# Loading wq before the keys, and summing P V's masked blocks on another engine

## The chip, the core and the metric

The kernel runs on one core of a Trainium2 chip. The core has a matrix engine (TensorE, PE in the profile, with its weight loads as PEld), a vector engine (VectorE, DVE), a scalar engine (ScalarE, ACT), a general engine (GpSimd, POOL) and a queue processor that here only issues transfers (SyncE, SP). Each engine runs its own list of instructions in order and waits on semaphores for the others. Sixteen DMA engines move data between the memory (HBM) and the on-chip memory. The metric is the device time of one execution in microseconds. A change of 0.2% is about 0.39 us.

## What is computed

One decode step of a transformer block for 8 sequences (B), one token each. x has 512 features. The layer norm of x is multiplied by wq into 32 query heads of 128 features. Each group of four query heads shares one of 8 key-value heads. Only the last 2048 of 8192 cached positions count:

```python
q = (layernorm(x) @ wq).reshape(8, 32, 128)
k = k_cache[:, :, -2048:, :]       # per sequence and kv head: 2048 x 128
v = v_cache[:, :, -2048:, :]
p = softmax(q . k * 128**-0.5)     # 4 query heads per kv head
h = x + (p . v).reshape(8, 4096) @ wo
# then a mixer/MLP block; for one token its token mixing adds zero:
y = layernorm(h); x1 = y
out = h + x1 + gelu(layernorm(x1) @ w3) @ w4
```

The keys and values that count are 2 x 64 x 2048 x 128 bf16 numbers, 67 MB; wq and wo are 4.2 MB each, w3 and w4 1.8 MB each. Each byte is used once.

## The kernel before

**Loads.** All loads but x go through SP's queue, in an order written out as a string in lines 776 to 785. A letter K loads one group of keys: four kv heads of one sequence, 2 MB, so that each sequence has two groups; V does the same for values. There are 16 groups of each, three buffers for keys (`knat`) and three for values (`vnat`). SP runs through the list in order; a load of K's group j first waits until group j - 3 has been turned (`e_Thi`), a load of V's group m until the products with group m - 3 are done (`e_PV`). A wait holds up everything behind it on SP. Q loads wq (`load_wq`, line 759): one transfer of nearly all of it into `wbig`, and six small ones (the last 1152 columns of every fourth row of wq, 18 to 72 KB each) into `wqF`. Four of the six wait for a memset of POOL (line 217). wo, w3 and w4 come at the end of the list; the last group of V goes into a buffer of K.

**Work per key group.** Keys must be turned so that features lie on partitions. `pe_T(i)` (line 381 on) does that for one item, a quarter of a group: eight PE transposes into PSUM. `evict(i)` copies the result to `kT_sb`, the lower half on ScalarE (line 393), the upper half on VectorE (line 395). `pe_QK(i)` multiplies it with the queries, two turns later. The main loop (line 613) goes over 64 items p: turn item p, score item p - 2, and at fixed distances behind the last item of a sequence the steps of its softmax, the products with V (`pe_PV`, two per sequence) and the output (`pe_O`). Before the loop stand the turns of the first four items (group 0) and then `q_rows` (x times wq) and `q_turn` (queries turned and copied to `qT`); `fill(0)` and `fill(1)` on POOL spread the queries of the first two sequences into `qblk`, which the scores need.

**Work per value group.** `pe_PV(m)` multiplies the weights of four kv heads with the values in sixteen matmuls. Each result row holds four blocks of 128 features of which only one belongs to it. For all but the last sequence VectorE multiplies the 128x512 bank with a 0/1 mask into `omask` (line 514), and two GpSimd adds fold the four blocks into one (`acc`, lines 516 and 517): first two pairs, then the rest. The last sequence has its own form on VectorE (lines 519 to 523). `pe_O` waits for both groups of a sequence and is issued four to five turns later. `omask` has one buffer, so the mask of the next group waits for the adds of the one before.

Of the kernel before, what the change touches and what calls it, by code (L numbers as in the profile page):

```python
# [8 lines left out]
ALU = mybir.AluOpType  # L9
AX = mybir.AxisListType  # L10
# [69 lines left out]
def bass_sequential_preLN__sliding_block_cached__mixer_s_mlp__decode_kernel(  # L80
# [23 lines left out]
    with es:  # L104
# [57 lines left out]
        omask = sb([128, NS, DH], dt.float32, "omask")  # L162
# [40 lines left out]
        PE, AC, DV, PO, SP = (Engine(S(n)) for n in ("s_pe", "s_act", "s_dve", "s_pool", "s_sp"))  # L203
# [25 lines left out]
        e = DV.op(lambda e: e.bn_stats(st6[:, :], x_sb[:, :]), X)  # L229
        e = DV.op(lambda e: e.bn_aggr(mv[:, :], st6[:, :]), e)  # L230
        e = PO.op(lambda e: e.tensor_scalar(rstd[:, :], mv[:, 1:2], EPS, None, ALU.add), e)
        e = PO.op(lambda e: e.tensor_tensor(rstd[:, :], rstd[:, :], half[0:B, 0:1], ALU.pow), e)
# [8 lines left out]
        e = DV.op(lambda e: e.tensor_reduce(hsq[:, :], ident_f[:, :].rearrange("p (u h) -> p h u", u=4), AX.X, ALU.add))  # L241
# [21 lines left out]
        e = PE.op(pe_xT, e_xln, e_idb)  # L263
# [14 lines left out]
        def q_rows():  # L278
            for k, rows, n, at, where in fills():
                a = xln_b[:, :]  # L280
                cols = bass.AP(tensor=a.tensor, offset=a.offset + KC * at + KC - 1, ap=[a.ap[0], [KC, k], [KC * k, 4]])
                e_xP = DV.op(lambda e, cols=cols, where=where: e.tensor_copy(
                    xlnP[:, where].rearrange("b (e a) -> b e a", a=4), cols))

            def pe_fT(e):
                for k, rows, n, at, where in fills():
                    ins = e.matmul(fT_ps[rows, n * B:(n + 1) * B], xlnP[:, where], ident_b[0:B, 0:B],
                                   is_transpose=True, tile_position=(0, rows.start))
                return ins
            e = PE.op(pe_fT, e_xP)  # L290
            for k, rows, n, at, where in fills():
                e_fT = DV.op(lambda e, rows=rows, n=n: e.tensor_copy(xlnF[rows, n, 0:B], fT_ps[rows, n * B:(n + 1) * B]),
                             e, e_fz)
            out = []
            for j in range(2):
                def pe_q(e, j=j):
                    for kc in range(KC):
                        for u in range(4):
                            n = (4 * j + u) * R * DH
                            size = R * DH if kc < KC - 1 else max(0, min(R * DH, H * DH - QF - n))  # L300
                            if size:
                                ins = e.matmul(S_ps[j][32 * u:32 * (u + 1), 0:size], xlnT[:, kc, :], wq_v[:, kc, n:n + size],  # L302
                                               start=(kc == 0), stop=(kc == KC - 1 and size == R * DH),
                                               tile_position=(0, 32 * u), skip_group_check=True)
                    return ins

                def pe_qF(e):
                    for n in range(NF):
                        for u in range(4):
                            w = (u - 4) * R * DH + QF  # L310
                            lo = max(0, -w)
                            if lo < R * DH:
                                ins = e.matmul(S_ps[1][32 * u:32 * (u + 1), lo:R * DH], xlnF[:, n, :],
                                               wqF[:, n, w + lo:w + R * DH], start=False, stop=(n == NF - 1),
                                               tile_position=(0, 32 * u), skip_group_check=True)
                    return ins
                e_q = PE.op(pe_q, e_xT, (sem_wq, 16))
                if j == 1:
                    e_q = PE.op(pe_qF, e_fT, (sem_wf, 16 * len(FILL)))
                got = S_ps[j][:, :].rearrange("p (r d) -> p r d", r=R)  # L320
                for c in range(2):
                    if j == 0:
                        e = AC.op(lambda e, c=c, got=got: e.activation(qrow2[:, 0, :, c, :], got, ACT.Copy, scale=inv_sqrt_dh),
                                  e_q)
                    else:
                        e = DV.op(lambda e, c=c, got=got: e.tensor_scalar(qrow2[:, 1, :, c, :], got, inv_sqrt_dh, None,
                                                                          ALU.mult), e_q)
                out.append(e)
            return out, e_q

        def q_turn():
            e_qT = []
            for j in range(2):
                def f(e, j=j):
                    for r in range(R):
                        ins = e.matmul(qT_ps[j][:, r * 128:(r + 1) * 128],
                                       qrow2[:, j, r, :, :].rearrange("p c d -> p (c d)").bitcast(dt.float32), ident_f[:, :],
                                       start=True, stop=True, is_transpose=True)
                    return ins
                e = PE.op(f, e_qrow[j], e_idf)  # L340
                got = qT_ps[j][:, :].bitcast(dt.bfloat16).rearrange("p (r u x) -> p r u x", r=R, u=4)[:, :, :, 0:2 * B]
                e_qT.append(DV.op(lambda e, j=j, got=got: e.tensor_copy(  # L342
                    qT[:, 4 * j:4 * (j + 1), :, :, :].rearrange("p u r b e -> p r u (b e)"), got), e))
            return e_qT[-1], e
# [10 lines left out]
        pool = [e_oz]  # L355
# [3 lines left out]
        e_acc, e_O, e_oX, e_oW = ({} for _ in range(4))  # L359
# [95 lines left out]
        free = {2: None}  # L455
# [41 lines left out]
        def pe_PV(m):  # L497
            b, q = divmod(m, NQ)
            at, bank = bank_of(q)

            def f(e):
                for n in range(NN):
                    u = n % 2
                    ins = e.matmul(bank[64 * u:64 * (u + 1), :],  # L504
                                   pT_sb[:, b % 2, n, :].rearrange("p (x q) -> p q x", q=NQ)[:, q, :],
                                   v_tile(m)[:, n * 512:(n + 1) * 512], start=(n < 2), stop=(n >= NN - 2),
                                   tile_position=(0, 64 * u), skip_group_check=True)
                return ins
            e_PV[m] = PE.op(f, V(m), *(e_pT[b, x] for x in range(KQ)), free[at])
            acc = oacc[:, b % 2, q, :]  # L510
            if b < LAST:
                a = own_s[:, :]
                own = bass.AP(tensor=a.tensor, offset=a.offset, ap=[a.ap[0], [1, NS], [0, DH]])
                free[at] = DV.op(lambda e: e.tensor_tensor(omask[:, :, :], bank.rearrange("p (s d) -> p s d", s=NS), own,  # L514
                                                           ALU.mult), e_PV[m], e_acc.get(m - 1), e_own_s)
                e = PO.op(lambda e: e.tensor_tensor(omask[:, 0:2, :], omask[:, 0:2, :], omask[:, 2:4, :], ALU.add), free[at], pool[-1])  # L516
                pool[-1] = e_acc[m] = PO.op(lambda e: e.tensor_tensor(acc, omask[:, 0, :], omask[:, 1, :], ALU.add), e, e_O.get(b - 2))  # L517
                return
            e = DV.op(lambda e: e.tensor_scalar(acc, bank[:, 0:DH], own_s[:, 0:1], None, ALU.mult),
                      e_PV[m], e_O.get(b - 2), e_own_s)  # L520
            for s in range(1, NS):
                e = DV.op(lambda e, s=s: e.scalar_tensor_tensor(acc, bank[:, s * DH:(s + 1) * DH], own_s[:, s:s + 1], acc,
                                                                ALU.mult, ALU.add), e)
            e_acc[m] = free[at] = e
# [74 lines left out]
        def quad(f, q):  # L599
# [3 lines left out]
                   (5, each(widen, 2)), (5, each(warm, 1)), (5, each(widen, 3)), (6, each(warm, 2)), (6, each(warm, 1))),  # L603
                  ((6, quad(pe_PV, 0)), (7, quad(pe_PV, 1)), (11, late_O), (8, last_O)))
        LAG = (0, 0, 0, 0, 0, 0, KQ, -1)
        for p in range(AHEAD):
            pe_T(p)
            evict(p)
        e_qrow, e_q = q_rows()
        e_qT, e_qturn = q_turn()  # L610
        fill(0)
        fill(1)
        for p in range(NITEM + 24):
# [160 lines left out]
                B_w4[lo * 128:hi * 128, :].rearrange("(g p k) n -> p g (k n)", p=128, k=k), sem_w4[n])  # L774

        turn = {"K": 0, "V": 0, "O": 0}
        for kind in "KQKK" + 9 * "VK" + "VKKVKVKVVVOVOO":
            if kind == "Q":
                load_wq()
                continue  # L780
            {"K": load_k, "V": load_v, "O": load_wo}[kind](turn[kind])
            turn[kind] += 1
# [42 lines left out]
```

## Time and profile before

| | us |
|---|---|
| median of 3 runs | 193.28 (193.27 to 193.34) |
| the profiled execution, its own time | 193.18 |
| its span, first to last instruction | 191.9 |
| busy: PE, DVE, ACT, POOL | 151.5, 102.5, 95.7, 30.3 |
| share of the span in which 16 DMA engines moved queue 1's data | 97.2% |
| read from HBM | 79.18 MB |

In the profile a row of the timeline gives the start, the length, the engine, the line of the kernel, the operation, output<-input, the number of instructions merged into it, and in brackets how long the engine was idle before it and what ended that. A row of a group ends with total busy time, mean ns of one instruction, and the idle time before them. SPq rows are issues of transfers: they last as long as SP needs to issue, not as long as the data flow. A row "0.00:2.00 ..." of the table by stretches gives, for that stretch, the busy time of each engine, the clock that was granted to TensorE (1.00 is full), the mean share of the DMA engines and the rate.

### The profile page before, as it was taken

How to read it: one execution, taken by the hardware profiler on the slowest of the kernel's cores; microseconds unless marked ns; L12 is line 12 of the kernel's file. 1: busy time of each engine (PE TensorE's matmuls, PEld its weight loads, DVE VectorE, ACT ScalarE, POOL GpSimd, SP SyncE). 2: the span in 40 equal slices, each digit the busy share in tenths (PEclk: the TensorE clock that was granted, in tenths of full speed). 3: DMA queues.
4: the chain of work that ended last, by engine and by line, in shares of the span. 5: the costliest groups of instructions: out<-in, count | busy, mean ns of one | idle time of the engine just before them, and what ended most of it. 6: DMA issues, size and time to landing. Idle time of an engine off the chain costs nothing.

```text
span 191.9 us, 3209 instructions
## 1 busy us (share of the span) xinstructions
PE 151.5 (79%) x1325; PEld 94.9 (49%) x1325; DVE 102.5 (53%) x245; ACT 95.7 (50%) x124; POOL 30.3 (16%) x65
## 2 busy tenths in 40 slices
PE   0293879988878998699978896989898994777874
PEld 0281247664546555465655463746554661323453
DVE  2754314773386438543775275646853885535323
ACT  3081127776272927284559263754782767420331
POOL 8300020100230023002300230024002200140030
PEclk9999769999996999889999997999999999999985
DMA  6999999999999999999999999999999999999991
GB/s 220 422 406 432 437 420 427 434 437 424 434 429 427 430 430 427 429 430 430 437 430 420 437 430 429 420 437 424 437 434 425 434 434 432 408 430 428 411 409 75
DMA packets 6478, 79.38 MB, mean 414 GB/s; under 512 B 688, under 2 KB 704, under 8 KB 1856
## 3 DMA queue, kind: packets, MB, share of 16 engines
q1 hardware_dynamic: 6448, 79.18, 97.2%
q8 instruction: 10, 0.16, 0.3%
q14 instruction: 4, 0.03, 0.0%
q10 hardware_dynamic: 16, 0.01, 0.0%
HBM read 79.18 MB, written 0.01 MB: 413 GB/s over the span
## 4 chain that ended last, share of the span: by engine, by line
DMA 65%; PE 22%; DVE 6%; ACT 4%; SPq 1%; issue 1%; POOL 0%
DMA knat<-in_A_k_cache_dram 31%; DMA w_sb<-in_B_w_dram 16%; DMA vnat<-in_A_v_cache_dram 10%; PE kT_ps L383 9%; DMA wbig<-in_A_wq_dram 8%; PE S_ps L504 3%; ACT pT_sb L472 2%; PE S_ps L408 2%; PE o_rows L504 2%; DVE kT_sb L395 2%; ACT kT_sb L393 1%; PE S_ps L302 1%; PE sm L529 1%; PE kT_ps L678 1%; SPq L207 1%
## 5 line engine op out<-in xcount | busy, mean ns | idle before, releaser
L393 ACT ACTIVATE kT_sb<-kT_ps 128x1024 bf16<-128x1024 bf16 x64 | 65.6, 1025 | 65.3 <-PE kT_ps L383 65.2
L383 PE MATMUL kT_ps<-turn_f,knat 128*128 128x128 f32 x512 | 76.5, 293 | 12.2 <-DMA knat<-in_A_k_cache_dram 9.6
L383 PEld LDWEIGHTS kT_ps<-turn_f,knat 128*128 128x128 f32 x512 | 60.4, 149 | 31.9 <-issue 13.4
L395 DVE COPY kT_sb<-kT_ps 128x1024 bf16<-128x1024 bf16 x64 | 43.9, 686 | 34.7 <-PE kT_ps L383 34.6
L516 POOL TENSOR_TENSOR omask<-omask 128x256 f32<-128x256 f32 x14 | 10.2, 726 | 113.3 <-DVE omask L514 113.3
L408 PE MATMUL S_ps<-kT_sb,qblk 128*32 128x512 bf16 x256 | 26.5, 408 | 1.7 <-POOL qblk L350 1.1
L504 PE MATMUL o_rows<-vnat,pT_sb 128*64 128x512 bf16 x128 | 15.4, 381 | 5.4 <-ACT pT_sb L472 5.4
L472 ACT ACTIVATE pT_sb<-o_rows,own_f 128x512 bf16<-128x512 f32 x28 | 17.7, 694 | 1.8 <-PE o_rows L467 1.6
L504 PE MATMUL S_ps<-vnat,pT_sb 128*64 128x512 bf16 x112 | 13.4, 382 | 0.7 <-DMA vnat<-in_A_v_cache_dram 0.7
L504 PEld LDWEIGHTS o_rows<-vnat,pT_sb 128*64 128x64 bf16 x128 | 8.0, 109 | 11.5 <-issue 7.7
L408 PEld LDWEIGHTS S_ps<-kT_sb,qblk 128*32 128x32 bf16 x256 | 6.6, 93 | 13.4 <-issue 8.3
L514 DVE TENSOR_TENSOR omask<-o_rows,own_s 128x512 f32<-128x512 f32 x7 | 4.8, 686 | 12.5 <-PE o_rows L504 12.5
L514 DVE TENSOR_TENSOR omask<-S_ps,own_s 128x512 f32<-128x512 f32 x7 | 4.8, 692 | 11.7 <-PE S_ps L504 11.7
L350 POOL COPY qblk<-qT 64x64 bf16<-64x64 bf16 x16 | 5.0, 312 | 27.0 <-DVE qT L342 16.4
L504 PEld LDWEIGHTS S_ps<-vnat,pT_sb 128*64 128x64 bf16 x112 | 5.8, 110 | 6.8 <-issue 1.6
L529 PE MATMUL sm<-oacc,sel_o 128*128 128x256 f32 x16 | 7.2, 537 | 0.6 <-DVE oX L536 0.6
L440 ACT ACTIVATE E_sb<-S_ps,negM 128x512 f32<-128x512 f32 x8 | 5.5, 689 | 2.4 <-DVE negM L436 2.4
L259 PE MATMUL sm<-ident_b,xln_b 8*128 8x8 bf16 x4 | 0.3, 176 | 8.0 <-DVE xln_b L234 8.0
L517 POOL TENSOR_TENSOR oacc<-omask 128x128 f32<-128x128 f32 x14 | 6.4, 455 | 1.1
L559 ACT ACTIVATE orow<-kT_ps 128x512 bf16<-128x512 f32 x1 | 0.6, 597 | 11.2 <-PE kT_ps L553 11.2
L431 DVE TENSOR_REDUCE mblk<-S_ps 128x1 f32<-128x512 f32 x8 | 5.5, 682 | 0.8 <-PE S_ps L408 0.8
L453 DVE STREAM_TRANSPOSE PT_sb<-P_sb 128x512 bf16<-128x512 bf16 x8 | 5.6, 702 | 0.0
(120 smaller groups left out, 102.6 us busy)
## 6 DMA issues: line engine op xcount, KB each, us to landing
knat<-in_A_k_cache_dram SPq DMA_DIRECT2D x16, 2048.0 KB, 19.3
vnat<-in_A_v_cache_dram SPq DMA_DIRECT2D x15, 2048.0 KB, 20.3
wbig<-in_A_wq_dram SPq DMA_DIRECT2D x1, 3808.0 KB, 16.1
wbig<-in_A_wo_dram SPq DMA_DIRECT2D x2, 1024.0 KB, 22.9
knat<-in_A_v_cache_dram SPq DMA_DIRECT2D x1, 2048.0 KB, 20.4
wbig<-in_A_wo_dram SPq DMA_DIRECT2D x1, 2048.0 KB, 24.7
w_sb<-in_B_w_dram SPq DMA_DIRECT2D x1, 1792.0 KB, 30.7
w_sb<-in_B_w_dram SPq DMA_DIRECT2D x1, 1024.0 KB, 32.6
```

Of the source, the lines that this page charges most:

```text
L383: ins = e.matmul(kT_ps[i % 2][:, n * 256:(n + 1) * 256].bitcast(dt.float32), knat[:, j % NK, c * DH:(c + 2) * DH].bitcast(dt.float32), tur ...
L393: e_lo[i] = AC.op(lambda e: e.activation(kT_sb[:, i % NKT, 0:W // 2], kT_ps[i % 2][:, 0:W // 2], ACT.Copy), e_Tlo[i], e_QK.get(i - NKT))
L395: e_hi[i] = DV.op(lambda e: e.tensor_copy(kT_sb[:, i % NKT, W // 2:W], kT_ps[i % 2][:, W // 2:W]), e_Thi[i], e_QK.get(i - NKT))
L408: ins = e.matmul(S_ps[b % 2][32 * t:32 * (t + 1), :], qblk[:, b % 2, KQ * q + t, half, at:at + H], kT[:, :, t, :, half], start=(q == 0 and ...
L431: e = DV.op(lambda e: e.tensor_reduce(mblk[:, 0:1], S_ps[b % 2][:, :], AX.X, ALU.max), e_QK[G * b + G - 1], e_mz)
L453: e_PT[b] = DV.op(lambda e: e.transpose(PT_sb[:, :], P_sb[:, :]), e_P[b], e_wide.get(b - 1))
L472: e_pT[b, t] = AC.op(lambda e: e.activation(pT_sb[:, b % 2, :, H * t:H * (t + 1)], bank[:, :].rearrange("p (n y) -> p n y", n=NN), ACT.Cop ...
L504: ins = e.matmul(bank[64 * u:64 * (u + 1), :], pT_sb[:, b % 2, n, :].rearrange("p (x q) -> p q x", q=NQ)[:, q, :], v_tile(m)[:, n * 512:(n ...
L514: free[at] = DV.op(lambda e: e.tensor_tensor(omask[:, :, :], bank.rearrange("p (s d) -> p s d", s=NS), own, ALU.mult), e_PV[m], e_acc.get( ...
L516: e = PO.op(lambda e: e.tensor_tensor(omask[:, 0:2, :], omask[:, 0:2, :], omask[:, 2:4, :], ALU.add), free[at], pool[-1])
L517: pool[-1] = e_acc[m] = PO.op(lambda e: e.tensor_tensor(acc, omask[:, 0, :], omask[:, 1, :], ALU.add), e, e_O.get(b - 2))
L529: e_O[b] = PE.op(lambda e: e.matmul(O_ps, sel_o[:, :], oacc[:, b % 2, :, :].rearrange("p q d -> p (q d)"), start=True, stop=True), e_acc[N ...
```

## The change

Two edits. First, the list of loads starts with Q instead of K, so that wq and its six small transfers are issued ahead of K's group 0, and in the program `q_rows` and `q_turn` are emitted ahead of the turns and evictions of the first four items; on PE, ScalarE and VectorE the work on q therefore stands first. The loads behind the first eight stay in their order. Second, the four masked blocks are added by one VectorE reduce, which reads `omask` with the block index innermost (steps of 512 bytes) and writes `acc`, in place of the two GpSimd adds. GpSimd's later work (the fills, a memset near the end) no longer stands behind those adds.

```diff
@@ pe_PV
-                e = PO.op(lambda e: e.tensor_tensor(omask[:, 0:2, :], omask[:, 0:2, :], omask[:, 2:4, :], ALU.add), free[at], pool[-1])
-                pool[-1] = e_acc[m] = PO.op(lambda e: e.tensor_tensor(acc, omask[:, 0, :], omask[:, 1, :], ALU.add), e, e_O.get(b - 2))
+                e_acc[m] = DV.op(lambda e: e.tensor_reduce(acc, omask[:, :, :].rearrange("p s d -> p d s"), AX.X, ALU.add),
+                                 free[at], e_O.get(b - 2))
@@ order of the first work
+        e_qrow, e_q = q_rows()
+        e_qT, e_qturn = q_turn()
         for p in range(AHEAD):
             pe_T(p)
             evict(p)
-        e_qrow, e_q = q_rows()
-        e_qT, e_qturn = q_turn()
         fill(0)
@@ order of the loads
-        for kind in "KQKK" + 9 * "VK" + "VKKVKVKVVVOVOO":
+        for kind in "QKKK" + 9 * "VK" + "VKKVKVKVVVOVOO":
```

## The prediction

> **What bounds the kernel now.** I read the page's slices first, then a table of busy time by stretches, then the end of the timeline, and only then the lines of the change.
>
> ```profile
> span 191.9 us, 3209 instructions
> ...
> PEclk9999769999996999889999997999999999999985
> DMA  6999999999999999999999999999999999999991
> GB/s 220 422 406 432 437 420 427 434 437 424 434 429 427 430 430 427 429 430 430 437 430 420 437 430 429 420 437 424 437 434 425 434 434 432 408 430 428 411 409 75
> ```
>
> Each digit is the busy share of one of 40 slices, in tenths. The DMA row is at nine tenths in every slice except the first and the last, and its rate never leaves 406 to 437 GB/s between them. The table by stretches (from:to, length, busy us of PE, PEld, DVE, ACT, POOL, granted clock, share of 16 DMA engines, GB/s) shows the same and gives the two ends:
>
> ```profile
> 0.00:2.00 2.00, 0.00 (x0) 0.00 (x0) 0.00 (x0) 0.67 (x1) 1.47 (x9) 1.00 0.01 4
> 2.00:4.00 2.00, 0.00 (x0) 0.00 (x0) 0.58 (x2) 0.82 (x2) 1.95 (x7) 1.00 1.08 377
> 4.00:32.00 28.00, 18.58 (x141) 12.14 (x141) 12.94 (x38) 8.43 (x10) 3.96 (x8) 0.88 1.00 422
> 32.00:184.00 152.00, 128.77 (x1066) 79.33 (x1064) 87.07 (x198) 83.19 (x107) 20.96 (x41) 0.97 1.01 429
> 184.00:186.00 2.00, 1.11 (x29) 0.93 (x28) 0.20 (x1) 1.58 (x2) 1.84 (x2) 0.91 1.02 419
> 186.00:188.00 2.00, 1.32 (x46) 1.26 (x47) 1.02 (x6) 0.50 (x2) 0.08 (x1) 0.50 0.82 327
> 188.00:189.00 1.00, 1.00 (x51) 0.97 (x43) 0.07 (x1) 0.00 (x0) 0.00 (x0) 0.50 0.27 104
> ```
>
> From 2 us to about 187 us all sixteen engines move data without a gap. In the first stretch no data flows yet (4 GB/s). The end of the timeline shows what the last work waits for:
>
> ```profile
> 185.08 1.98 PE L678 MATMUL kT_ps<-uT,w_sb 128*128 128x8 bf16 x56 [0.89 <-DMA w_sb<-in_B_w_dram]
> ...
> 189.36 0.14 PEld L731 LDWEIGHTS S_ps<-w_sb,qrow 128*32 128x32 bf16 x8 [0.21 <-DMA w_sb<-in_B_w_dram]
> ```
>
> PE waits 0.89 us for w3 and 0.21 us for the last piece of w4. So the time is: 2 us until data flows, the bytes at 429 GB/s, and 2.5 us behind the last landing (189.36 to 191.9). The change moves no byte out of the kernel. It can move the time only by delaying the first byte, by leaving the DMA queue empty at some point, or by making the computing so late that w3 and w4 are no longer what the end waits for.
>
> **The change, part one: order of the loads and of the first work.** The rows of the first 33 us: SP's issues, the one POOL memset that a load waits for, and PE.
>
> ```profile
> 0.72 0.64 SPq L207 DMA_DIRECT2D knat<-in_A_k_cache_dram  x1
> 1.42 0.57 SPq L207 DMA_DIRECT2D wbig<-in_A_wq_dram  x1
> 2.03 4.55 SPq L207 DMA_DIRECT2D w_sb<-in_A_wq_dram  x6
> ...
> 14.21 0.54 SPq L207 DMA_DIRECT2D knat<-in_A_k_cache_dram  x1
> ...
> 32.24 0.54 SPq L207 DMA_DIRECT2D knat<-in_A_k_cache_dram  x1
> ```
> ```profile
> 0.94 2.02 POOL L217 MEMSET w_sb<- 64x2304 bf16 x1
> ```
> ```profile
> 8.59 5.60 PE L383 MATMUL kT_ps<-turn_f,knat 128*128 128x128 f32 x32 [0.26 <-DVE turn_f L239]
> 15.48 0.23 PE L287 MATMUL sm<-ident_b,xlnP 8*32 8x8 bf16 x6 [1.29 <-DVE xlnP L282]
> 17.57 2.85 PE L302 MATMUL S_ps<-wbig,xlnT 128*32 128x512 bf16 x30 [1.86 <-DMA wbig<-in_A_wq_dram]
> 20.35 1.46 PE L313 MATMUL S_ps<-w_sb,xlnF 64*32 64x128 bf16 x9
> 21.74 0.66 PE L336 MATMUL o_rows<-ident_f,w_sb 128*128 128x128 f32 x4
> 23.20 0.66 PE L336 MATMUL sm<-ident_f,w_sb 128*128 128x128 f32 x4 [0.80 <-DVE w_sb L326]
> 24.99 0.90 PE L408 MATMUL S_ps<-kT_sb,qblk 128*32 128x512 bf16 x8 [1.13 <-POOL qblk L350]
> 25.82 1.97 PE L383 MATMUL kT_ps<-turn_f,knat 128*128 128x128 f32 x8
> ```
>
> SP's queue: wq is issued at 0.72 instead of 1.42, the six small loads follow at once. Four of them wait for the memset, done at 0.94 + 2.02 = 2.96; the third would now be reached at about 0.72 + 0.57 + 2 x 0.76 = 2.8 (0.76 is 4.55 / 6), so it waits some 0.1 us. K's group 0 is issued behind all seven, at about 6.0; groups 1 and 2 and V's first follow as before, at most 0.1 us later. By then wq's 4.19 MB (512 x 4096 x 2 bytes) are still flowing until 2 + 4.19 / 0.429 = 11.8. No gap. Cost at the first byte: between -0.07 us (wq's issue took 0.57, K's 0.64, if the flow starts when the issue ends) and 0; I take 0.
>
> PE: wq now lands without 2.10 MB of K ahead of it: 17.57 - 2.10 / 0.429 = 12.7. The chain from the first product to the end of q's last turn took 23.86 - 17.57 = 6.3, so it ends near 19.0. K's group 0 now has 4.19 MB ahead of it: 8.59 + 9.8 = 18.4 as the lower bound. The small loads sit between, and may drain unevenly; before, the products that use them started at 20.35 without a wait, 2.8 us behind wq's landing, so they cost K at most 2.8 us: upper bound 21.2. I take the lower end, which q's chain covers: the turns of group 0 start at 19.0 and take 5.60 as before, so they end at 24.6 instead of 14.2.
>
> Who waits for those turns? SP: the load of K's group 3 reuses group 0's buffer, and V's second load is queued behind it. It went out at 14.21 and now goes out at 24.6. The queue then holds wq, three groups of K and one of V, 4.19 + 4 x 2.10 = 12.58 MB. From the table above exactly that much had flowed by 32.0 (2 x 4 + 2 x 377 + 28 x 422 kB/us). From an issue to its data pass about 1.3 us (0.72 to 2). So the load must go out by 30.7; it has 6.1 us to spare, where it had 16.5. Cost 0, and the cover is named: 6.1 us of queued loads. Beyond it every microsecond costs a microsecond.
>
> Scores, then K's items 4 to 7: before, scores of 0 and 1 started at 24.99, waiting for q. Now q's blocks are ready near 20 and they start when the turns end, 24.6. The four turns behind them ran from 25.82 to 32.2 (the issue of the next group at 32.24 marks it), so now to about 31.9. From here the order of work is the old one, 0.3 us early; the queue by then reaches to 32.0 + 9.8 = 41.8. Nothing of the head start survives, and nothing is lost.
>
> **Part two: the sum over the masked blocks.** Fourteen times (b < 7) two GpSimd adds go and one VectorE reduce of 128x512 to 128x128 comes, which reads in steps of 512 bytes.
>
> ```profile
> L516 POOL TENSOR_TENSOR omask<-omask 128x256 f32<-128x256 f32 x14 | 10.2, 726 | 113.3 <-DVE omask L514 113.3
> L517 POOL TENSOR_TENSOR oacc<-omask 128x128 f32<-128x128 f32 x14 | 6.4, 455 | 1.1
> ```
> ```profile
> L431 DVE TENSOR_REDUCE mblk<-S_ps 128x1 f32<-128x512 f32 x8 | 5.5, 682 | 0.8 <-PE S_ps L408 0.8
> ```
> ```profile
> L542 DVE TENSOR_REDUCE oW<-oX 128x32 bf16<-128x128 f32 x8 | 3.1, 389 | 0.3
> ```
> ```profile
> 92.06 0.69 DVE L514 TENSOR_TENSOR omask<-S_ps,own_s 128x512 f32<-128x512 f32 x1 [1.49 <-PE S_ps L504]
> 93.08 0.69 DVE L395 COPY kT_sb<-kT_ps 128x1024 bf16<-128x1024 bf16 x1 [0.33 <-PE kT_ps L383]
> ```
> ```profile
> 95.95 0.33 PE L383 MATMUL kT_ps<-turn_f,knat 128*128 128x128 f32 x1 [0.31 <-DVE kT_sb L395]
> ```
> ```profile
> 146.47 1.92 PE L504 MATMUL S_ps<-vnat,pT_sb 128*64 128x512 bf16 x16 [0.65 <-DMA vnat<-in_A_v_cache_dram]
> ```
> ```profile
> 173.17 1.92 PE L504 MATMUL S_ps<-knat,pT_sb 128*64 128x512 bf16 x16 [1.63 <-DMA knat<-in_A_v_cache_dram]
> ```
>
> Removed: 14 x (726 + 455) ns = 16.5 us of POOL. Nobody waited for it (the products of O come four turns later); worth 0. Added on VectorE: between 0.68 us each (as many elements reduced from PSUM, L431) and 4 x 389 = 1.56 us (L542's strided reduce, four times the elements). I take 0.71, L542 plus 384 more elements at L431's slope over a 128-element reduce (about 0.83 ns each); 14 x 0.71 = 10 us in all. Behind the second block of a pair the reduce runs from 92.75 to 93.49, so the eviction of 93.08 starts 0.41 us later, the maximum and its short chain follow, and the 0.31 us that PE waits at 95.95 become 0.72. That is +0.4 us of PE per b, six times. The first block's delay lies beside the 1.92 us of the next P V. Its cover: PE waits for data again before each next pair, last at 146.47 (0.65 us) and 173.17 (1.63 us, V's last group), and 0.89 us more ahead of w3. So the delay of one b, at most 1.3 us at the upper price, is gone before the end. Cost 0.
>
> **Sum.** 0 + 0 + 0 against the profiled execution's 193.18 us (the span, and 1.3 us around it); the median shown is 193.28, 0.05% above. Forecast 193.2.
>
> **The rivals.** *K's group 3 comes too late (slower).* It decides at an issue after 30.7. In the trace a turn took 1.97 us at 25.82, in the slice where the granted clock was 0.6, behind a stretch in which PE had stood much of the time; the new order leaves PE with next to nothing to do until 12.7. Four turns at that rate are 7.9 us: 19.0 + 7.9 = 26.9, and from the late landing 21.2 + 7.9 = 29.1, both in time. Only with an eviction (0.69 us, as at 93.08) in series behind each turn, 21.2 + 4 x 2.66 = 31.8, does the queue run dry, for 1.1 us: 194.3. Chance 0.09: about half of it for turns at that slow rate, since the granted clock has fallen behind idle stretches in this trace, the rest for a delay that no row shows.
>
> The Trainium skill, "TensorE: Matmul & The Clock Gate", Part 1, says that PE's clock is halved behind one idle window of some 3.4 us, and it speaks against this change: by it all four turns may run at half rate, end at 26.9 and leave 3.8 us to spare instead of 6.1, with the time still 193.2. The slices at 0.7 and 0.6 agree with it as far as they go.
>
> *VectorE becomes the bound (slower).* Two b's delays must outlast 0.65 + 1.63 + 0.89 us with the first of them drained at 146.47: 2 x d > 3.2, d > 1.6, a reduce above 1.9 us. Both bounds above lie under it. At 2.5 us: d = 2.2, 4.4 - 3.2 = +1.2, 194.4. Chance 0.04.
>
> *The engines end differently (either sign).* They don't finish together: 0.82 x 2 + 0.27 x 1 = 1.9 us of work for all sixteen would have been done at 187.9, and the last piece is awaited until 189.36. Where the small loads sit could change who is behind. Evener by a third of that 1.4 us: 192.7; as much less even: 193.7. Against it: each engine has the same bytes in both orders. Chances 0.15 and 0.08.
>
> *The change doesn't do what it says:* q's products do come 5 us earlier, but the first scores don't, as shown; that is in the forecast.
>
> **How the numbers follow.** No change 0.64, late group 0.09, VectorE 0.04, ends 0.15 and 0.08. 0.2% of 193.28 is 0.39 us, about what a measurement of this kernel can tell from no change. Faster 0.15, same 0.64, slower 0.21. The likeliest case alone spans 192.9 to 193.7. The range 192.6 to 194.3 takes in the uneven ends and the milder half of the two slow cases and leaves out some 0.13.
>
> **What would show it.** Right: wq's products start near 12.7 and K's first turns near 19; the third reload of K leaves near 25 and the slices of DMA stay at nine tenths; L514 is followed by a reduce of about 0.7 us; PE's wait for VectorE behind it grows from 0.3 to 0.7 us; w3 is still awaited near 185.1. Wrong: a DMA slice between 25 and 40 us under nine tenths, a w3 that PE does not wait for, or another last landing of w4 at equal bytes.

## The result and the profile after

The changed kernel took 193.03 us (median of 22 runs, 192.83 to 193.34) against 193.34 for the kernel before (22 runs, 193.18 to 193.52): a ratio of 0.9984, 95% interval 0.9978 to 0.9990, so 0.3 us less. A second comparison gave the same: 193.04 against 193.31, ratio 0.9985 (0.9977 to 0.9994). That lies within the 0.2% that was called no change, but the whole interval lies below 1, so the gain is small and not only scatter. The profiled execution took 193.02 us. Ratios here and below rest on the undisturbed runs, so they can differ from the quotient of the medians.

The page of the changed kernel, with its span and the two rows of DMA slices:

```profile
span 191.7 us, 3167 instructions
...
DMA  6999999999999999999999999999999999999991
GB/s 231 458 394 427 434 427 434 427 426 424 434 434 431 431 427 434 422 424 431 438 438 424 431 431 431 424 431 429 431 434 431 424 434 431 421 431 419 413 404 64
```

No slice between the ends falls under nine tenths. The table by stretches of the changed kernel, in the same columns as before:

```profile
0.00:2.00 2.00, 0.00 (x0) 0.00 (x0) 0.00 (x0) 0.66 (x1) 1.47 (x9) 1.00 0.62 156
2.00:4.00 2.00, 0.00 (x0) 0.00 (x0) 0.59 (x2) 0.83 (x2) 1.95 (x7) 1.00 0.84 320
4.00:32.00 28.00, 18.75 (x153) 12.43 (x153) 13.61 (x39) 9.55 (x11) 3.95 (x8) 0.94 0.99 422
32.00:184.00 152.00, 127.59 (x1046) 77.98 (x1052) 100.27 (x210) 81.84 (x106) 4.41 (x13) 0.96 1.01 429
...
186.00:188.00 2.00, 1.32 (x47) 1.26 (x49) 1.10 (x6) 0.50 (x2) 0.31 (x1) 0.63 0.71 280
188.00:189.00 1.00, 1.00 (x48) 0.86 (x36) 0.00 (x0) 0.00 (x0) 0.00 (x0) 0.50 0.16 59
```

From 4 to 184 us the rates are those of before, 422 and 429 GB/s. What differs is the start: 156 GB/s in the first 2 us where there were 4, and by 4 us 0.95 MB (2 x 156 + 2 x 320 kB) against 0.76. These 0.19 MB are 0.4 us of flow at 429 GB/s. Correspondingly less is left at the end: 280 and 59 GB/s behind 186 us against 327 and 104. Stretches of 0.2 us show when data begin to move (a packet is booked whole in one stretch, hence shares above 1; the 41 GB/s ahead of K's data are 8 KB, the size of x). First the kernel before, then the changed one:

```profile
1.60:1.80 0.20, 0.00 (x0) 0.00 (x0) 0.00 (x0) 0.20 (x1) 0.20 (x1) 1.00 0.13 41
1.80:2.00 0.20, 0.00 (x0) 0.00 (x0) 0.00 (x0) 0.20 (x1) 0.20 (x1) 1.00 0.00 0
2.00:2.20 0.20, 0.00 (x0) 0.00 (x0) 0.00 (x0) 0.20 (x1) 0.20 (x1) 1.00 2.35 573
```
```profile
1.60:1.80 0.20, 0.00 (x0) 0.00 (x0) 0.00 (x0) 0.20 (x1) 0.20 (x1) 1.00 2.17 498
1.80:2.00 0.20, 0.00 (x0) 0.00 (x0) 0.00 (x0) 0.20 (x1) 0.20 (x1) 1.00 4.08 1066
```

The flow begins about 0.4 us earlier when wq is the first transfer. The timeline of the changed kernel, SP's issues and the steps of PE that the prediction spoke of:

```profile
0.72 0.40 SPq L207 DMA_DIRECT2D wbig<-in_A_wq_dram  x1
1.17 4.74 SPq L207 DMA_DIRECT2D w_sb<-in_A_wq_dram  x6
5.95 1.92 SPq L207 DMA_DIRECT2D knat<-in_A_k_cache_dram  x3
...
25.16 0.54 SPq L207 DMA_DIRECT2D knat<-in_A_k_cache_dram  x1
...
30.79 0.54 SPq L207 DMA_DIRECT2D knat<-in_A_k_cache_dram  x1
```
```profile
12.31 3.59 PE L302 MATMUL S_ps<-wbig,xlnT 128*32 128x512 bf16 x30 [1.50 <-DMA wbig<-in_A_wq_dram]
...
19.33 5.80 PE L383 MATMUL kT_ps<-turn_f,knat 128*128 128x128 f32 x32 [0.62 <-DMA knat<-in_A_k_cache_dram]
25.06 0.62 PE L408 MATMUL S_ps<-kT_sb,qblk 128*32 128x512 bf16 x8
...
184.86 1.98 PE L678 MATMUL kT_ps<-uT,w_sb 128*128 128x8 bf16 x56 [0.45 <-DMA w_sb<-in_B_w_dram]
```
```profile
189.19 0.14 PEld L731 LDWEIGHTS S_ps<-w_sb,qrow 128*32 128x32 bf16 x8 [0.24 <-DMA w_sb<-in_B_w_dram]
```

SP issued wq in 0.40 us, where it had issued K's first group in 0.64. w3 comes 0.22 us earlier (184.86 against 185.08), the last piece of w4 0.17 us (189.19 against 189.36), and PE still waits for both, so the data still set the end. The two profiled executions differ by 0.16 us, the medians by 0.31; single runs of one kernel scatter by 0.2 to 0.3 either way.

The second part of the change: the group of the reduce, and what PE waits for at the turns (total us, times, longest):

```profile
L516 DVE TENSOR_REDUCE oacc<-omask 128x128 f32<-128x512 f32 x14 | 14.9, 1062 | 0.5
```
```profile
PE kT_ps L383 <- DMA knat<-in_A_k_cache_dram: 9.6, 10, 1.7
PE kT_ps L383 <- DVE kT_sb L395: 4.9, 13, 0.6
```

One reduce takes 1.06 us. The place behind a second block, in the timeline of the changed kernel:

```profile
51.84 0.69 DVE L514 TENSOR_TENSOR omask<-S_ps,own_s 128x512 f32<-128x512 f32 x1 [1.22 <-PE S_ps L504]
...
52.56 1.07 DVE L516 TENSOR_REDUCE oacc<-omask 128x128 f32<-128x512 f32 x1
...
53.56 0.68 DVE L395 COPY kT_sb<-kT_ps 128x1024 bf16<-128x1024 bf16 x1
...
56.41 0.33 PE L383 MATMUL kT_ps<-turn_f,knat 128*128 128x128 f32 x1 [0.55 <-DVE kT_sb L395]
```

The eviction of the turned keys goes straight behind the reduce, and PE waits up to 0.6 us for it. PE has that time: it still waits 9.6 us in all for keys, ten times.

### The profile page after: what moved, and what is told of

Read it like the earlier page. It is cut to its first block, busy times and chain, and to the rows that moved or that the text cites. A ratio compares the mean times of both kernels' runs of the same rounds, so it can differ in the third digit from the quotient of the medians.

```text
span 191.7 us, 3167 instructions
## 1 busy us (share of the span) xinstructions
PE 150.8 (79%) x1318; PEld 93.8 (49%) x1325; DVE 116.5 (61%) x259; ACT 95.5 (50%) x124; POOL 13.7 (7%) x37
## 4 chain that ended last, share of the span: by engine, by line
DMA 66%; PE 18%; DVE 6%; ACT 5%; SPq 2%; POOL 1%; issue 1%; POOLq 0%
DMA knat<-in_A_k_cache_dram 39%; DMA w_sb<-in_B_w_dram 16%; DMA vnat<-in_A_v_cache_dram 11%; PE kT_ps L383 9%; ACT pT_sb L472 2%; SPq L207 2%; PE o_rows L504 2%; ACT kT_sb L393 2%; PE S_ps L504 2%; DVE kT_sb L395 2%; PE S_ps L408 2%; DVE oacc L516 1%; PE kT_ps L678 1%; POOL w_sb L217 1%; PE S_ps L731 1%
## 5 line engine op out<-in xcount | busy, mean ns | idle before, releaser
L383 PEld LDWEIGHTS kT_ps<-turn_f,knat 128*128 128x128 f32 x512 | 59.0, 146 | 35.8 <-DMA knat<-in_A_k_cache_dram 13.3
L504 PE MATMUL o_rows<-vnat,pT_sb 128*64 128x512 bf16 x128 | 17.1, 412 | 5.5 <-ACT pT_sb L472 5.5
L516 DVE TENSOR_REDUCE oacc<-omask 128x128 f32<-128x512 f32 x14 | 14.9, 1062 | 0.5
L504 PE MATMUL S_ps<-vnat,pT_sb 128*64 128x512 bf16 x112 | 14.0, 393 | 0.9 <-DMA vnat<-in_A_v_cache_dram 0.9
L504 PEld LDWEIGHTS o_rows<-vnat,pT_sb 128*64 128x64 bf16 x128 | 8.5, 117 | 12.4 <-issue 9.1
L323 ACT ACTIVATE w_sb<-S_ps 128x512 bf16<-128x512 f32 x2 | 1.1, 594 | 11.4 <-PE S_ps L302 11.4
L529 PE MATMUL sm<-oacc,sel_o 128*128 128x256 f32 x16 | 6.1, 466 | 0.6 <-DVE oX L536 0.6
L431 DVE TENSOR_REDUCE mblk<-S_ps 128x1 f32<-128x512 f32 x8 | 5.4, 679 | 0.8 <-PE S_ps L408 0.8
```

The costliest lines, as they stand in the source:

```text
L383: ins = e.matmul(kT_ps[i % 2][:, n * 256:(n + 1) * 256].bitcast(dt.float32), knat[:, j % NK, c * DH:(c + 2) * DH].bitcast(dt.float32), tur ...
L431: e = DV.op(lambda e: e.tensor_reduce(mblk[:, 0:1], S_ps[b % 2][:, :], AX.X, ALU.max), e_QK[G * b + G - 1], e_mz)
L504: ins = e.matmul(bank[64 * u:64 * (u + 1), :], pT_sb[:, b % 2, n, :].rearrange("p (x q) -> p q x", q=NQ)[:, q, :], v_tile(m)[:, n * 512:(n ...
L516: e_acc[m] = DV.op(lambda e: e.tensor_reduce(acc, omask[:, :, :].rearrange("p s d -> p d s"), AX.X, ALU.add), free[at], e_O.get(b - 2))
L529: e_O[b] = PE.op(lambda e: e.matmul(O_ps, sel_o[:, :], oacc[:, b % 2, :, :].rearrange("p q d -> p (q d)"), start=True, stop=True), e_acc[N ...
```

## The experiments

My theory after the result: the start of the flow is the whole gain, the reduce is hidden, and the new order of the program is what keeps the new order of the loads from costing time. Rivals: the sum on VectorE brings the gain (GpSimd out of the way); the gain lies in how the engines end. Each kernel is the kernel before with the edit shown, unless another is named. Times before stand beside each since they were measured with it.

**The order alone.**

```diff
+        e_qrow, e_q = q_rows()
+        e_qT, e_qturn = q_turn()
         for p in range(AHEAD):
...
-        e_qrow, e_q = q_rows()
-        e_qT, e_qturn = q_turn()
...
-        for kind in "KQKK" + 9 * "VK" + "VKKVKVKVVVOVOO":
+        for kind in "QKKK" + 9 * "VK" + "VKKVKVKVVVOVOO":
```

> Only the first part: Q first in the list of loads and q's work first in the program; GpSimd keeps its two adds. Early start (the first transfer's issue is short, so the data flow starts some 0.3 us sooner and everything behind it moves): -0.3 us against the kernel before, 193.0, with data flowing before 2.0 us. Uneven ends (which engine is behind at the end has changed by chance): anything between -0.5 and +0.5. VectorE's sum as the cause: 0, 193.3.

193.07 us against 193.23, ratio 0.9990 (0.9981 to 0.9998). Its flow and its end, from the table by stretches and the timeline:

```profile
1.80:2.00 0.20, 0.00 (x0) 0.00 (x0) 0.00 (x0) 0.20 (x1) 0.20 (x1) 1.00 4.86 1219
```
```profile
184.90 1.26 PE L678 MATMUL kT_ps<-uT,w_sb 128*128 128x8 bf16 x33 [0.76 <-DMA w_sb<-in_B_w_dram]
```

Data flow before 2.0 us and w3 comes at 184.90, near the 184.86 of the changed kernel, without the reduce. The wait there is 0.76 us instead of 0.45: with the reduce, the work comes to this point later, but not too late.

**The sum alone.**

```diff
-                e = PO.op(lambda e: e.tensor_tensor(omask[:, 0:2, :], ...
-                pool[-1] = e_acc[m] = PO.op(lambda e: e.tensor_tensor(acc, ...
+                e_acc[m] = DV.op(lambda e: e.tensor_reduce(acc, omask[:, :, :].rearrange("p s d -> p d s"), AX.X, ALU.add),
+                                 free[at], e_O.get(b - 2))
```

> Only the second part: VectorE's reduce in place of the two GpSimd adds, old order of loads and work. Early start: 0, 193.3, with data flowing from 2.2 us as before. VectorE's sum as the cause: -0.3, 193.0. My own step: the reduce costs about 1.06 us each (measured in the changed kernel), PE's wait for VectorE grows, the time stays.

193.24 us against 193.23, ratio 1.0000 (0.9991 to 1.0009). Its waits of PE:

```profile
PE kT_ps L383 <- DMA knat<-in_A_k_cache_dram: 6.8, 7, 1.7
PE kT_ps L383 <- DVE kT_sb L395: 4.9, 13, 0.6
```

Waits for VectorE rose from 2.2 us in all in the kernel before to 4.9, and waits for keys fell from 9.6 to 6.8: one wait takes the place of the other, +2.7 against -2.8. The sum brings nothing and costs nothing that these runs can tell, and the gain belongs to the order (0.16 us by medians with the order alone, 0.31 with both parts; the intervals of the two ratios overlap).

**The loads alone, the program as before.**

```diff
-        for kind in "KQKK" + 9 * "VK" + "VKKVKVKVVVOVOO":
+        for kind in "QKKK" + 9 * "VK" + "VKKVKVKVVVOVOO":
```

> Only the list of loads begins with Q; in the program the turns of K's group 0 stay ahead of q's work, so PE stands until group 0 lands near 19.3, turns it until 25, and only then makes q (6 us). K's group 4 is then issued near 38 to 39, where the queue reaches to about 41.5. Early start: -0.3, 193.0, since the queue just holds. If my account of the queue is too kind by 2 us, the DMA runs dry near 41 and it is slower than before.

195.11 us (193.9 to 196.42) against 193.23, ratio 1.0090 (1.0059 to 1.0122). SP's issues, and the table by stretches:

```profile
24.74 0.54 SPq L207 DMA_DIRECT2D knat<-in_A_k_cache_dram  x1
...
39.24 0.53 SPq L207 DMA_DIRECT2D knat<-in_A_k_cache_dram  x1
```
```profile
36.00:40.00 4.00, 4.00 (x38) 2.81 (x37) 2.08 (x3) 3.07 (x3) 0.00 (x0) 1.00 1.00 430
40.00:44.00 4.00, 4.00 (x38) 2.81 (x36) 2.60 (x7) 3.07 (x3) 0.62 (x2) 1.00 0.83 315
```

Here q's work stood behind group 0's turns and began at 26, though wq had long landed, so the scores and the turns of items 4 to 7 came late and the load that waits for them went out at 39.24 instead of 32.24. The queue ran short: 4 x (434 - 315) = 476 kB against the same stretch of before, or 1.1 us. w3 came at 186.84, and the last piece of w4 later still:

```profile
191.25 0.14 PEld L731 LDWEIGHTS S_ps<-w_sb,qrow 128*32 128x32 bf16 x8 [0.28 <-DMA w_sb<-in_B_w_dram]
```

The table by stretches places most of the rest there. Shares of 0.99 from 186 to 188 us, 0.73 in the next microsecond and 0.21 in the one after are 2.9 us of work for all sixteen engines, which would have been done at 188.9; the last piece is awaited 2.3 us longer, where that was 1.5 us in the kernel before. So the engines also finished less evenly; why they did was not tested.

**The program alone, the loads as before.**

```diff
+        e_qrow, e_q = q_rows()
+        e_qT, e_qturn = q_turn()
         for p in range(AHEAD):
...
-        e_qrow, e_q = q_rows()
-        e_qT, e_qturn = q_turn()
```

> Only the program's order: q's work ahead of the turns of K's group 0, loads as before (K first). Group 0 has landed at 8.5 but is turned only behind q, from 24 to 29.6, so its buffer's next load is issued near 29.6 where I reckoned 30.7 as the last moment. Early start: 0, 193.3, flow from 2.2 us as before, queue just not dry. If the last moment is earlier than I reckoned: up to +1 us.

193.30 us, ratio 1.0025 (1.0001 to 1.0049): seven of twelve runs lie between 193.17 and 193.31, the others reach up to 195.69. In the profiled one of 193.20 us PE's turns and SP's load behind them:

```profile
23.71 4.38 PE L383 MATMUL kT_ps<-turn_f,knat 128*128 128x128 f32 x32
```
```profile
28.12 0.54 SPq L207 DMA_DIRECT2D knat<-in_A_k_cache_dram  x1
```

A load at 28.12 is in time: the stretches up to 44 us show 422 to 442 GB/s. It is probably near the edge (below), and turns at a slower clock would pass it, but none of the long runs was profiled. Their mean granted clock is no lower (0.946 in the two longest, 0.938 to 0.955 in the seven short ones), so the scatter stays open. This kernel has no early flow (nothing from 1.8 to 2.0 us) and no gain.

**K's first group in two halves**, to make the first transfer of the kernel before a smaller one, and **wq in two pieces** on top of the new order, for the same question.

```diff
+            if j == 0:
+                for lo in (0, 16):
+                    dma(SP, knat[4 * lo:4 * lo + 64, 0, :], ...
+                return
```

> The kernel before with nothing changed but K's group 0 loaded as two halves of 64 partitions, K still ahead of wq. Early start by a shorter first issue (before: 0.64 us and data from 2.17; wq first: 0.40 and data from 1.9): the first half's issue should be shorter than 0.64, data flow before 2.0 us, and the time fall by 0.1 to 0.3 us, with no change of order at all. If it is the place of wq itself (its long rows, or K behind it) that pays: 0, 193.25.

```diff
-            dma(SP, wbig[:, 0:size], ...
+            for lo, hi in ((0, 16), (16, 128)):
+                dma(SP, wbig[lo:hi, 0:size], ...
```

> The order of the changed kernel with GpSimd's two adds, and wq's first transfer cut into a head of 16 partitions and the rest of 112. Early start, if the issue lasts by the number of rows: head issued in less than 0.40 us, data from 1.7 to 1.8, another -0.1 against the changed order alone, 192.95. If the first issue has a floor near 0.4 us: the same as the changed order alone, 193.05.

K's halves gave six runs from 197.42 to 206.29 us (median 200.51, ratio 1.0255, 1.0209 to 1.0300; the profiled one took 201.32), wq in two pieces 200.88 us (ratio 1.0388, 1.0375 to 1.0402). From 4 to 32 us, the one, then the other:

```profile
4.00:32.00 28.00, 13.06 (x97) 8.58 (x97) 10.85 (x35) 5.16 (x6) 3.69 (x8) 0.87 1.01 315
```
```profile
4.00:32.00 28.00, 11.37 (x82) 6.89 (x83) 9.47 (x33) 3.71 (x5) 3.96 (x8) 1.00 0.97 318
```

The DMA engines are as busy as ever (1.01 and 0.97) but move 315 and 318 GB/s instead of 422: some 107 GB/s less over 28 us, 3.0 MB, or 7 us. Cutting the first transfer by partitions made the engines slow, so these two times tell nothing of a first transfer's size. The Trainium skill, "SBUF — State Buffer", "Door 1: The DMA port swizzle", says that the rate goes by how many of 16 ports the partitions reach, and that 64 neighbouring ones reach eight. The halved group agrees with that (210 GB/s in the page's second slice, up to 9.6 us, where the kernel before has 422); that the full transfers queued behind it were slow as well, the section does not say.

The start of the two does bear on the question. The issues of the halves, then those of the two pieces of wq with their first data:

```profile
0.72 1.32 SPq L207 DMA_DIRECT2D knat<-in_A_k_cache_dram  x2
```
```profile
0.72 0.84 SPq L207 DMA_DIRECT2D wbig<-in_A_wq_dram  x2
```
```profile
1.60:1.80 0.20, 0.00 (x0) 0.00 (x0) 0.00 (x0) 0.20 (x1) 0.20 (x1) 1.00 1.74 193
```

Half a group of keys was not issued faster (0.66 us on average against 0.64 for a whole one), and its data came no sooner (15 GB/s from 1.8 to 2.0 us). Nor did 16 partitions of wq start sooner than 128: 0.42 us on average, and data from the stretch 1.6 to 1.8 us in both. Both expectations of an earlier start are refuted.

**The rival that VectorE becomes the bound**, on the changed kernel: the reduce done twice and three times (the same values are written again).

```diff
-                e_acc[m] = DV.op(lambda e: e.tensor_reduce(acc, ...
+                e = free[at]
+                for _ in range(3):
+                    e = DV.op(lambda e: e.tensor_reduce(acc, ...
+                e_acc[m] = e
```

> The changed kernel with each VectorE reduce done three times over (3.2 us instead of 1.06 per group of V; the result is the same). By my rival's working the point from which VectorE decides is a reduce of 1.9 us: each b then delays PE by d = 3.2 - 0.3 = 2.9 us, and two b's exceed the 3.2 us of waits by about 2.6: 195.6 instead of 193.0. If PE's other waits take up more than I counted: 193.0 to 194.

> The changed kernel with each VectorE reduce done twice (2.1 us per group of V; same result). By my rival's working, with the point at 1.9 us: d = 1.8, 2 x 1.8 - 3.2 = +0.4, 193.4. By the reading of the run with three reduces (each b loses the second block's d and what of the first block's 0.69 + 2.12 outlasts 2.3 us of scores and P V, 0.5, and gets back 9.6 / 7 = 1.4 us of waits for data; six times): 6 x (1.8 + 0.5 - 1.4) = +5.4, 198.4.

Three times: 211.7 us, ratio 1.0933 (1.0892 to 1.0974). Twice: 193.22 us against 193.35, ratio 0.9994 (0.9986 to 1.0003). Waits of PE, with three reduces (the profiled run of 213.61 us, the longest of its six) and then with two (193.89 us, the longest of its eleven):

```profile
PE kT_ps L383 <- DVE kT_sb L395: 21.1, 14, 2.8
...
PE kT_ps L383 <- DMA knat<-in_A_k_cache_dram: 2.0, 1, 2.0
```
```profile
PE kT_ps L383 <- DVE kT_sb L395: 11.7, 13, 1.5
...
PE kT_ps L383 <- DMA knat<-in_A_k_cache_dram: 5.9, 6, 2.0
```

At 2.1 us per group 5.9 us of waits for keys are left and the time hardly moves. At 3.2 us they are all but gone (2.0 us, once), so every delay reaches the loads, and the rate falls in the page's slices to as little as 247 GB/s. The point lies between 2.1 and 3.2 us. My rival had put it at 1.9, and by its working the threefold reduce gives 195.6; it gave 211.7. Below the point its working was nearly right (193.4 for the double reduce), and the other reading written down for that run, 198.4, is refuted. Above the point the price was far too low: 18.5 us for 1.06 us more in each of 14 groups (14.9 us) is more than the work that was added. The threefold kernel's mean granted clock was also lower (0.88 to 0.89 in its six runs, 0.94 in the changed kernel's profiled run), so PE's own work may have taken part of that; how much was not measured.

**The changed kernel again.**

> The changed kernel once more, beside the others on the same chip. Early start: 193.0, as the changed order alone (193.07), since the reduce is worth 0; 0.16% below the kernel before.

The result is given at the top.

**Why does the flow begin earlier?** Three kernels, all on the order alone. wq described in 32 x 4 rows instead of 128:

```diff
-            dma(SP, wbig[:, 0:size], A_wq.rearrange("(p k) n -> p (k n)", k=KC)[:, 0:size], sem_wq)
+            dma(SP, wbig[:, 0:size], A_wq.rearrange("(a t k) n -> a t (k n)", t=4, k=KC)[:, :, 0:size], sem_wq)
```

> The changed order alone (GpSimd's two adds stay), with wq's large transfer described as 32 times 4 rows, as K's groups are, in place of 128 rows. The same rows go to the same partitions. Early start by a short first issue: the issue takes about 0.6 us instead of 0.40, data flow from about 2.1 instead of 1.8, and the time is back near 193.25. If the gain comes from wq's place or its long rows and not from the issue: 193.05, as the changed order alone. If the description makes no difference to the issue (0.40 us), the run says nothing on this.

193.06 us against 193.35, ratio 0.9985 (0.9976 to 0.9993). The issue still took 0.40 us, so by what was written ahead it says nothing. Then x, which ScalarE issues, moved to SP's queue behind wq:

```diff
-        dma(AC, x_sb[:], A_x.rearrange("b s d -> (b s) d"), sem_x)
...
             dma(SP, wbig[:, 0:size], ...
+            dma(SP, x_sb[:], A_x.rearrange("b s d -> (b s) d"), sem_x)
```

> The changed order alone, with x issued by SP behind wq instead of by ScalarE at the same moment as wq. If two issues at once share what makes the descriptors, wq's engines start sooner and closer together: -0.1 to -0.2, 192.9. If each queue issues on its own: 193.05, the small loads 0.6 us later, at no cost.

193.89 us (193.18 to 195.21) against 193.35, ratio 1.0039 (1.0017 to 1.0061). wq's issue (0.39 us) and the early flow stayed. The loss is elsewhere: PE's first work, SP's load, and the table by stretches:

```profile
15.35 0.29 PE L258 MATMUL sm<-ident_b,xln_b 8*128 8x8 bf16 x4 [15.35 <-DVE xln_b L233]
```
```profile
29.20 0.54 SPq L207 DMA_DIRECT2D knat<-in_A_k_cache_dram  x1
```
```profile
28.00:32.00 4.00, 3.98 (x37) 2.66 (x35) 2.08 (x3) 2.79 (x4) 0.00 (x0) 1.00 0.92 377
32.00:36.00 4.00, 4.00 (x37) 2.88 (x36) 2.08 (x3) 3.01 (x4) 0.00 (x0) 1.00 0.95 369
```

x is 8 KB, but behind wq its layer norm is ready at 15.35 instead of 8.02. The load of K's group 3 then leaves at 29.20 and the flow thins to 377 and 369 GB/s. With 28.12 in time (the program alone) and 29.20 too late, the last moment lies between them, as an estimate: the flows of the two kernels began some 0.4 us apart.

The third cuts wq into pieces that keep all 128 partitions:

```diff
-            dma(SP, wbig[:, 0:size], ...
+            rows, own = A_wq.rearrange("(p k) n -> p k n", k=KC), H * DH - QF
+            dma(SP, wq_v[:, :, 0:own], rows[:, :, 0:own], sem_wq)
+            dma(SP, wq_v[:, 0:KC - 1, own:H * DH], rows[:, 0:KC - 1, own:H * DH], sem_wq)
```

> The new order of loads and work, GpSimd's adds kept, with wq moved by two transfers: first the first 2944 columns of each of the four rows that a partition holds (128 x 4 pieces of 5.9 KB, 3.0 MB), then the other 1152 columns of three of the rows (128 x 3 pieces of 2.3 KB, 0.9 MB). All 128 partitions are in both, and the bytes are the same; only the first transfer now has as many pieces as a group of keys (512) instead of 128 long ones. Two theories of the earlier start of the flow. The number of pieces: SP needs 0.6 us for the first issue, as for K's, and data flow only from about 2.0 to 2.2 us; the time loses what the order had won, 193.3 us beside 193.3 for the kernel before. wq itself (where it lies in memory, whatever its pieces): issue 0.40 us, flow from 1.8 us on, and the time stays at 193.05. In either case K's group 0 is issued some 0.5 us later, behind a queue of 4.2 MB, which costs nothing.

194.07 us against 193.33, ratio 1.0041 (1.0027 to 1.0054). Its issues and the first flow:

```profile
0.72 1.34 SPq L207 DMA_DIRECT2D wbig<-in_A_wq_dram  x2
```
```profile
1.80:2.00 0.20, 0.00 (x0) 0.00 (x0) 0.00 (x0) 0.20 (x1) 0.20 (x1) 1.00 0.00 0
2.00:2.20 0.20, 0.00 (x0) 0.00 (x0) 0.00 (x0) 0.20 (x1) 0.20 (x1) 1.00 0.63 88
...
2.00:4.00 2.00, 0.00 (x0) 0.00 (x0) 0.58 (x2) 0.82 (x2) 1.95 (x7) 1.00 0.85 209
```

With wq cut, the two issues took 0.67 us each on average, and no data of wq flow before 2.0 us, as with K first. So the early start does not go with wq as such, but with the shape of the first transfer. It is not the number of pieces, though: what was written down ahead had that wrong. A group of keys is not 512 pieces but 128 of 16 KB, one to a partition (64 positions of one head lie together). The page of the kernel before has too few packets for 32 groups of 512:

```profile
DMA packets 6478, 79.38 MB, mean 414 GB/s; under 512 B 688, under 2 KB 704, under 8 KB 1856
```

So first transfers of 16 and of 128 pieces started early (wq), and those of 64, 128 and 512 late (half a group of keys, a group, the cut wq). Two differences are left. The early pieces are long (29.75 KB each, against 16 and 5.9 KB). And they are laid out more simply: one to a partition, at one even distance in memory, whereas K's lie at two distances and the cut wq's come four to a partition. No run separates these, so why the flow begins earlier stays open.

The theory's time was missed too: 193.3 was expected, and the other 0.8 us lie right behind the start. From 2 to 4 us this kernel moved 209 GB/s where the one before moved 377, 0.34 MB less or 0.8 us, and from 4 to 32 us as much as it, 422; why these pieces start so slowly stays open. It does support the account of the gain: the time follows the bytes moved by 4 us in both directions, 0.19 MB more and 0.31 us shorter in the changed kernel, 0.34 MB less and 0.74 us longer here.

## Why the prediction was right, and the term that was off

The forecast was 193.2 us and no change as the likeliest case, and 193.03 with -0.16% is that, inside the likeliest case's own range of 192.9 to 193.7. The sum, however, was 0 + 0 + 0, and one of its terms was not 0. That the result still lies in the range is in part luck: the range reached down to 192.9, while the bounds of the sum's own terms gave no reason for less than 193.1.

- **First byte (mis-sized).** "Cost at the first byte: between -0.07 us [...] and 0; I take 0." It was -0.4 us in the flow (0.19 MB by 4 us), which accounts for the 0.31 us gained at the end. The lower end was wrong because it came from wq's issue as the second transfer (0.57 us). As the first it takes 0.40, and the start of the data moved by more than the issue did (0.24). The rows of before could not show this; the bound should have been wider.
- **q's chain.** Predicted 12.7 to 19.0, measured 12.31 to 18.7 (the last step at 18.05 + 0.66). The wq products took 3.59 us instead of 2.85, and the next step 0.82 instead of 1.46, so that two errors of the chain nearly cancel. A low clock after PE had stood still would explain the first, but the profile prints a granted clock of 1.00 from 12 to 16 us, so that is not shown.
- **K's turns.** "I take the lower end" (18.4) for the landing: it was 19.33, PE waiting 0.62 us for it, so q's chain did not cover it quite. Turns to 25.06 instead of 24.6, the load out at 25.16 instead of 24.6. Within 0.6 us at each step.
- **The spare time.** "So the load must go out by 30.7": the runs put this between 28.1 and 29.2, so the spare was some 3 to 4 us and not 6.1. I had counted the queue as one; the DMA engines need not run dry together, which is an argument and was not measured. The step still held.
- **The late group (rival, 0.09).** Its mechanism is real: it is what the loads alone showed, only one group further on (the load for group 4, at 39.24). In the full change the program's order takes it away. Its price of a slow clock did not come: the four turns took 5.80 us, not 7.9. By the Trainium skill, "TensorE: Matmul & The Clock Gate", Part 1, the turns could have run at half rate behind the idle start; the trace agrees for their first part only (granted clock 0.50 from 20 to 22 us, 1.00 from 23 us on). wq's products took 3.59 us against 1.90 where PE came straight from other work (the loads alone), which would fit half a clock, but as said the profile prints 1.00 there.
- **The reduce.** "I take 0.71" with bounds of 0.68 and 1.56; it took 1.06 us. Adding elements at the slope of neighbouring ones to a small strided reduce was too cheap. The Trainium skill, "SBUF — State Buffer", "Door 1: The DMA port swizzle", notes that each access that moves to a new line of 16 bytes costs extra; reading in steps of 512 bytes does so each time, and 1.06 us against 0.68 for as many neighbouring elements (L431) agrees with it, though L431 is a maximum that reads PSUM and writes one number per partition, so the pair is not clean. PE's wait behind it was up to 0.6 us where 0.7 was predicted, which is in part luck: with 1.06 us the same working gives 0.31 + 0.41 + 0.35 = 1.07. The cover named for it, waits for data, held, and shrank by 2.8 us in the kernel with the sum alone.
- **Different ends (rival, 0.15 and 0.08).** The gain has the sign of the more likely half of this rival, but not its mechanism. Less work is left behind 186 us (0.71 x 2 + 0.16 = 1.6 us of sixteen engines against 1.9), because all of it started earlier, and the last piece is awaited 0.17 us sooner. The ends are no more even than before: that work would be done at 187.6, 1.6 us ahead of the last piece (189.19), where it was 1.5. In the loads alone, and there to its loss, the mechanism does show (2.3 us).

## What to carry to other kernels

In a kernel whose DMA queue never runs dry, a new order of the same transfers can win time only at its two ends: look when the first bytes move, and try another transfer as the first one. Here wq's long rows ahead of a group of keys brought the data 0.4 us sooner. A new order of loads must come with the matching order of the program, since the engines run in order and a load that waits for a buffer is held up by whatever stands ahead of the work that frees it; here the loads alone lost 1.9 us, and loads and program together won 0.16. Work moved to another engine is free as long as waits for data remain behind it, and the loss is steep once they are used up.

## What was not expected of the hardware

- The data of the kernel began to move about 0.4 us earlier with wq as the first transfer (128 pieces of 29.75 KB, issue 0.40 us) than with a group of keys (128 of 16 KB, 0.64 us). With wq cut into shorter pieces they began as late as with the keys. The same wq took 0.57 us to issue as the second transfer.
- Transfers on 64 or on 16 and 112 partitions at the head of the queue brought the flow from 422 to 315 and 318 GB/s over 28 us with all engines busy, full transfers behind them included.
- A transfer of 8 KB behind one of 3.9 MB on the same queue had its result ready 7.3 us later than from a queue of its own (15.35 against 8.02).
- A strided sum of 128x512 to 128x128 in steps of 512 bytes took 1.06 us on VectorE; a sum to 128x32 from a quarter of the elements took 0.39, and a maximum over as many neighbouring elements from PSUM 0.68.
